# One-bank slot reads, two states loaded through GpSimd's queue, and a first layer fed head group by head group

## The chip, the cores and the metric

The kernel runs on one core of one Trainium2 chip. The core has TensorE (PE in the profile, with its weight loads as PEld), VectorE (DVE), ScalarE (ACT), GpSimd (POOL), SyncE (SP) and 16 DMA engines that all queues share. The metric is the device time of one execution in microseconds (us); lower is better.

## The reference, cut to what matters

Two stages follow each other. The first is an attention between 512 tokens and 32 state slots, for 8 batches and 8 heads of 64 numbers, read in both directions; the second is a two-layer perceptron over all 4352 rows that the first stage gives (8 batches of 512 tokens and 32 slots, 512 wide).

```python
scores  = scale * x @ state.T          # per batch and head: 512 x 32
a       = softmax(scores)              # over the 32 slots
xread   = a @ state                    # 512 x 64
scores2 = scale * state @ x.T          # 32 x 512
a2      = softmax(scores2)             # over the 512 tokens
sread   = a2 @ x                       # 32 x 64: the slot reads
rows    = concat(xread, sread)         # 544 rows a batch, heads side by side: 512 wide
h       = rows @ w_in                  # 512 -> 2048
g       = s * relu(h)**2 + b
out     = g @ w_out                    # 2048 -> 512
```

## The kernel before, in words

**Tiling.** Four heads lie together on the 128 partitions (32 slots each), in two groups g. Heads 2q+g belong to group g, so the two groups are the even and the odd heads. The token reads are never formed: since `xread @ w_in` is `a @ (state @ w_in)`, the kernel makes M = state x w_in for each batch and each quarter c of w_in (`att_M`; eight matmuls on tiles of 64 rows by 32 columns, then a cast of the 128x1024 result from PSUM to fp16 by ACT or DVE), and the first layer (`layer1`) multiplies M by the normalised scores a4. One "h" step of `layer1` is four matmuls into one pair of PSUM banks (two blocks f, and for each the two groups g), then a relu by ACT and a square by DVE. `layer2` works on sums and differences of blocks (`pair_sums` on the activations, `weight_sums` on w_out) in seven steps of eight parts; batch 0 goes through `layer2_first` without them.

**Scores.** For batch 0 x arrives in four pieces (`x0_load`, SP's queue), each piece is cast, transposed on TensorE and copied back; the states of batch 0 (`stf[0]`) and of batches 1 and 2 (`stf[1]`) come by two DMAs issued from ACT at lines 411 and 412, are cast by DVE (`att_st`) and transposed on TensorE. Score matmul, exp, a matmul with a block of ones for the sum over slots (D), ln, exp and a DVE product then give a4, for each group by itself. From batch 3 on a4 is made in another way: SP transposes exp(scores) by DMA into aT, DVE normalises it (`att_divide`) and SP transposes it back.

**Slot reads.** `part_V` (line 730) forms `a2 @ x` of one batch from aT and x: for each group, each of four token blocks c and each of four column parts q there are two matmuls, one for token rows 0 to 63 and one for rows 64 to 127, on tiles of 64x32, 64 columns long, into two PSUM banks. That is 64 matmuls. ACT or DVE copies the first bank (`vt`), DVE adds the second (line 930) and multiplies by the reciprocal of the sum (line 936). SP transposes the result, POOL copies it to its place, and `layer1_slots` uses all batches together near the end.

**Order.** Nothing is ordered by a scheduler at run time: the table TURNS lists, for each of the five engines, the numbers of its operations in the order in which they are issued, and every engine works through its own list strictly in order. `Plan.order` merges the lists, chooses buffers, and puts idle matmuls on a zero tile (`fill`) into TensorE's modelled gaps in the first 20 us. Its durations and landing times are a model's inputs, not measurements. TensorE changes between three modes: full (128x128), tiled (64x32) and cols (128x32).

**Loads.** After a copy that waits for the small constant, POOL issues the large loads one after the other: w_in part 1, w_in part 0, x of batch 1, w_in 2, w_out 0, w_in 3, w_out 1, x of batch 4, w_out 2, w_out 3, x of batch 2. At most eight such loads are under way; the ninth waits for the first.

Of the kernel before, what the change touches and what calls it, by code (L numbers as in the profile page):

```python
# [10 lines left out]
FP32 = mybir.dt.float32  # L11
# [7 lines left out]
        26 28 24 34 30 32 47 35 38-39 57 59 49 83 86 80 178 77 180 65 51 67 182 89 92 106-107 118 114 186  # L19
        108 119 110-111 71 112 115-116 185 120 113 98 117 126 95 109 122 230 127 123 227 124 215 128-129 221  # L20
        125 224 142-144 138-139 73 101 140-141 218 145 121 130 158 236 104 154-157 159-161 134 75 69 135 131
        136-137 132 54 1044 323 133 150 146 62 147 233 260 326-327 151 261 251 148 262 152 252 149 253 263
        153 254 162 264 255 163 350 166 265 167 338 344 256 164 266 1051 267 168-169 332 257-258 165 341 353
        270-272 687 438 273 347 335 279-281 274-275 282 276-277 1058 560 443 283-286 288-292 447 445 689 293
        298 294 299 295 300-304 563 569 441 308-312 305 313-315 565 1065 682 377 368-369 378-379 370-372 380
        373 381-382 472 454 374-375 383 475 469 384 387 460 388-391 463 392-393 457 396-400 394 401-403 1079
        567 685 405-412 415 466 416 425-426 582 427 585 417-418 579 419-421 428-429 1072 932 430 422 588 594
        431 490 432 597 591 491-492 499 576 500 707 493 501 494-496 502-503 497 504-505 691 804 928 506
        509-516 518-522 527 523-524 528 813 925 529 525 530-534 704 537 547-550 538-539 551 540 713 552 541
        553 719 542 701 554 543-544 716 621 698 612-614 622 615 623-624 616-619 710 625 838 626 631 627 841  # L30
        628 930 934 632-635 640 636-638 641-643 811 807 649 644-645 650 646 651 647 652-656 809 1086 1093
        659 669-671 660 672 661 673-674 662-663 675 820 664-665 676 835 826 734-738 666 829 739 743 740 744
        741 832 745-749 753-754 750 755-758 947 759-760 762-763 823 764-766 771-773 767-769 774-776 950 781
        777 782-783 778 784-788 791-794 956 953 856-857 795 858 796 859 797 944 798 860 1110 861 865-866 962
        867 941 862 868 863 1105 869-870 875 871-872 876-879 1115 880-881 884 882 885-889 893-894 890
        895-896 891 959 897-899 903-906 900 907 1100 908-910 913-919 1120 920 1130 977-978 1125 1135 986
        979-982 987 983-984 988-992 996 993 997-1003 1005-1011 1014 1012 1015-1021 1024-1031 1034-1041
        1152-1159 1161-1168 1171-1178 1180-1187 1189-1196 1199-1206 1209-1216
    """,
    "ACT": """  # L40
        27 29 21 36 33 37 40 43 41 44 60 84 87 81 78 66 183-184 90 93 190-191 72 187-188 99 96 231 228 216
        222 225 74 102 219 237 70 55 1046 325 324 63 328-329 234 351 339 345 333 342 354 688 440 439 348 336
        444 561-562 448 690 446 564 570 442 1067 683-684 566 473 455 476 470 461 458 464 686 467 568 586 583
        580 933 589 595 592 598 708 577 805-806 929 814 692 926-927 714 705 720 702 717 699 711 839 931 935
        842 808 812 1095 810 821 836 830 827 833 948 824 951 957 954 945 963 942 1111 1116 1108 1106 960
        1113 1103 1101 1121 1123 1118 1131 1136 1126 1128 1133 1138
    """,
    "DVE": """
        19-20 23 46 25 22 31 48 58 42 45 61 50 179 88 181 79 68 53 52 82 91 85 192 205 94 189 6 203 207 217
        229 7 223 204 100 1045 232 97 103 226 245 242 220 105 170 172 76 209 56 1047 64 238-239 208 318 199  # L50
        1048 1052 330 240 200 235 210 243 248-249 241 202 213 250 211 352 1059 1053 176 1054 206 259 174
        1055 246 268 212 244 201 343 340 355 334 214 349 278 1060 247 1061 337 287 1062 450-451 296 452 306
# [3 lines left out]
        587 489 1080 816 610 817-818 555 545 721 706 603 709 608 601 718 620 700 1083 712 715 604 731 629  # L56
# [5 lines left out]
        1160 1142 1169 1151 1179 1188 1148 1197 1207 1217  # L62
    """,
    "POOL": """
        8 10 9 15 12 11 14 13 437 16-18 197 193 195 322 559 171 269 317 307 803 386 681 414 177 175 424 536
        434 556 508 546 678 1078 173 297 1064 1085 1050 668 1092 1099 1057 1071 752 630 874 658 902 912 800
        780 922 790
    """,
# [229 lines left out]
def kernel(  # L298
# [10 lines left out]
    nc = tc.nc  # L309
# [414 lines left out]
    def V_bank(b, m):  # L724
        return T(("V", b))[:, m]
# [696 lines left out]
```

## Time and profile before

| what | value |
|---|---|
| median of the runs shown | 210.18 us (208.64 to 210.22, 3 runs) |
| the profiled execution | 209.36 us, of which its span is 207.6 us |
| PE, DVE, ACT, POOL busy, share of the span | 97%, 79%, 55%, 18% |
| first matmul of the first layer | 14.63 us from the span's start |
| last matmul | ends at 203.58 us |

The span runs from the first to the last instruction of the profiled execution; what lies around it makes the rest of its time. Times in views count from the span's start. A busy TensorE here is one with matmuls in its pipeline, so small steps can be stretched without showing as idle.

### The profile page before, as it was taken

Reading aid. Unit: us, or ns where it says so; the run is one execution under the profiler, and the core shown is the slowest. Engines: PE = TensorE matmul, PEld = TensorE weight load, DVE = VectorE, ACT = ScalarE, POOL = GpSimd, SP = SyncE. Lnnn points to the kernel's source line nnn. Section 1 sums busy time; section 2 is a strip of 40 time slices with the busy share of each in tenths; the row PEclk is TensorE's granted clock in tenths of the full one; section 3 lists DMA queues with packets and bytes.
Section 4 is the critical chain, followed back from the end, with each engine's and each line's share of the span. In section 5 each row is a group of like instructions: output and inputs, shape, how many; then the busy total and the mean of one; then the engine's idle time right before and its main releaser. Section 6 shows DMA issues by size and latency. Waiting matters only on the chain.

```text
span 207.6 us, 5286 instructions
## 1 busy us (share of the span) xinstructions
PE 200.6 (97%) x2240; PEld 136.3 (66%) x2240; DVE 164.6 (79%) x334; ACT 114.0 (55%) x158; POOL 37.6 (18%) x59
## 2 busy tenths in 40 slices
PE   7799999999999999999999999999999999999992
PEld 4655444446557685676568756686777778888881
DVE  3466836979999879888989979996798756899671
ACT  3468987656577986548675595743532541340000
POOL 5821002010030040302100230003750002160000
PEclk9999999999999999999999999999999999999998
DMA  5999999979999749999902255004402003152054
GB/s 167 228 205 203 204 205 155 181 140 141 175 131 209 132 104 180 113 178 217 195 0 54 101 100 165 3 3 106 164 6 101 3 0 103 54 176 81 0 192 113
DMA packets 47768, 25.87 MB, mean 125 GB/s; under 512 B 32128, under 2 KB 45952, under 8 KB 47744
## 3 DMA queue, kind: packets, MB, share of 16 engines
q0 software_dynamic: 13744, 15.21, 36.6%
q1 hardware_dynamic: 33056, 10.10, 25.8%
q8 instruction: 17, 0.28, 0.6%
q10 hardware_dynamic: 944, 0.23, 0.5%
q14 instruction: 7, 0.06, 0.1%
HBM read 17.33 MB, written 8.91 MB: 126 GB/s over the span
## 4 chain that ended last, share of the span: by engine, by line
PE 93%; DMA 3%; DVE 1%; ACT 0%; ACTq 0%; issue 0%
PE o L336 50%; PE pair L336 43%; DMA stf<-in_state_dram 3%; ACT M L425 0%; DVE st L425 0%; DVE xn L425 0%; ACTq L411 0%; DVE osb L1273 0%; ACTq L410 0%; DVE stT L425 0%
## 5 line engine op out<-in xcount | busy, mean ns | idle before, releaser
L999 ACT ACTIVATE g<-pair 128x1024 f16<-128x1024 f32 x64 | 63.5, 1023 | 41.5 <-PE pair L336 41.2
L336 PE MATMUL pair<-a,M 128*128 128x512 f16 x256 | 63.9, 379 | 0.5 <-ACT M L425 0.5
L336 PEld LDWEIGHTS <-pd 128*128 128x128 f16 x480 | 46.3, 98 | 10.9 <-issue 2.3
L336 PEld LDWEIGHTS <-g 128*128 128x128 f16 x424 | 40.7, 98 | 18.4 <-issue 2.6
L1005 DVE TENSOR_TENSOR g<-g 128x1024 f16<-128x1024 f16 x64 | 42.5, 687 | 2.7 <-ACT g L999 2.7
L336 PE MATMUL o<-u,pd 128*128 128x256 f16 x360 | 44.4, 273 | 0.0
L336 PE MATMUL o<-wo,g 128*128 128x256 f16 (+1 forms) x272 | 42.9, 285 | 0.0
L336 PEld LDWEIGHTS <-M 128*128 128x128 f16 x256 | 24.7, 98 | 23.0 <-ACT M L425 1.0
L1176 POOL DMA_DIRECT2D out_dram<-osb x28 | 18.9, 744 | 98.9 <-DVE osb L1284 55.8
L1273 DVE SCALAR_TENSOR_TENSOR osb<-o,s,bias_bc 128x512 f32<-128x512 f32 (+1 forms) x32 | 22.9, 716 | 12.6 <-PE o L336 11.2
L425 ACT CAST M<-pair 128x1024 f16<-128x1024 f32 x24 | 23.6, 1015 | 9.6 <-PE pair L336 9.4
L1284 DVE SCALAR_TENSOR_TENSOR osb<-o,s,osb 128x512 f32<-128x512 f32 (+1 forms) x24 | 17.2, 715 | 7.5 <-PE o L336 7.2
L1085 DVE TENSOR_TENSOR pd<-g 128x1024 f16<-128x1024 f16 (+1 forms) x32 | 20.4, 651 | 0.1
L336 PE MATMUL o<-wo,pd 128*128 128x256 f16 x120 | 17.9, 273 | 0.0
L336 PE MATMUL o<-u,g 128*128 128x256 f16 x120 | 17.5, 273 | 0.0
L1096 DVE TENSOR_TENSOR pd<-g,pd 128x512 f16<-128x512 f16 (+1 forms) x32 | 12.8, 400 | 0.0
L1093 DVE TENSOR_TENSOR pd<-g,pd 128x512 f16<-128x512 f16 (+1 forms) x32 | 12.3, 402 | 0.1
L780 ACT ACTIVATE E<-pair 128x512 f16<-128x512 f32 x16 | 9.4, 598 | 3.1 <-PE pair L336 3.1
L466 POOL DMA_DIRECT2D xn<-in_x_dram x7 | 6.6, 949 | 22.8 <-ACT vt L425 10.7
L336 PE MATMUL pair<-wo,g 128*128 128x512 f16 x32 | 10.5, 380 | 0.0
L1046 ACT ACTIVATE g<-pair 128x256 f16<-128x256 f32 x16 | 5.2, 386 | 9.0 <-PE pair L336 9.0
L336 PE MATMUL pair<-wi,stT 64*32 64x512 f16 x224 | 10.0, 382 | 0.0
(72 smaller groups left out, 147.7 us busy)
## 6 DMA issues: line engine op xcount, KB each, us to landing
out_dram<-osb POOLq DMA_DIRECT2D x28, 256.0 KB, 3.4
xn<-in_x_dram POOLq DMA_DIRECT2D x7, 512.0 KB, 10.7
wi<-in_moe_w_in_dram POOLq DMA_DIRECT2D x4, 512.0 KB, 9.1
wo<-in_moe_w_out_dram POOLq DMA_DIRECT2D x4, 512.0 KB, 19.4
u<-in_x_dram SPq DMA_DIRECT2D x4, 256.0 KB, 4.2
out_dram<-osb SPq DMA_DIRECT2D x4, 256.0 KB, 2.7
out_dram<-osb SPq DMA_DIRECT2D x4, 128.0 KB, 2.3
pd<-in_state_dram SPq DMA_DIRECT2D x1, 320.0 KB, 3.8
```

Of the source, the lines that this page charges most:

```text
L336: return nc.tensor.matmul(out, lhsT, rhs, start=start, stop=stop, tile_position=tp, is_transpose=is_transpose, skip_group_check=True,)
L425: (nc.scalar.copy if e == "ACT" else nc.vector.tensor_copy)(dst, src)
L466: lambda e: nc.gpsimd.dma_start(out=T(xn[b]).rearrange("p h c d -> p h (c d)"), in_=x[b].rearrange("h (q c) d -> q h (c d)", q=P),),
L780: nc.scalar.activation(T(E[b])[:, g, :].rearrange("p (m t) -> p m t", m=2), T(u)[:, :, hS * g : hS * g + hS], AF.Exp, scale=scale, accum_o ...
L999: lambda e, u=u, part=part: nc.scalar.activation(part(), T(u), AF.Relu),
L1005: lambda e, part=part: nc.vector.tensor_mul(part(), part(), part()),
L1085: nc.vector.tensor_tensor(view()[:, :, 0:2], blocks(b, j)[:, :, 1:2, :].to_broadcast((P, 2, 2, n)), blocks(b, j)[:, :, 0:4:3, :], ALU.subt ...
L1093: nc.vector.tensor_tensor(view()[:, :, 2], blocks(b, j)[:, :, 3], view()[:, :, 0], ALU.subtract)
L1096: nc.vector.tensor_tensor(view()[:, :, 3], blocks(b, j)[:, :, 2], view()[:, :, 2], ALU.subtract)
L1176: lambda e: eng(e).dma_start(dst, src()),
L1273: lambda e: nc.vector.scalar_tensor_tensor(t_view(u), o_view(bank), s_bc, bias(h), ALU.mult, ALU.add),
L1284: lambda e: nc.vector.scalar_tensor_tensor(t_view(u), o_view(bank), s_bc, t_view(u), ALU.mult, ALU.add),
```

## The change

Four things are changed in the code, and the TURNS table is rewritten for all engines.

1. **Slot reads.** `part_V` drops the split of the token rows: 32 matmuls over all 128 rows on tiles of 128x32, into one bank. The copy into `vt` and the addition fall away (16 instructions in 8 batches), and the product with the reciprocal reads PSUM directly.
2. **States of batches 1 and 2.** The DMA for `stf[1]` leaves ACT's queue (line 412) and becomes an operation of POOL's list, behind w_in 0.
3. **Order of the loads.** POOL's list becomes w_in 0, `stf[1]`, x of batch 1, w_in 1, w_out 0, w_in 2, w_out 1, w_in 3, w_out 2, w_out 3, x of batch 2, x of batch 3. The x of batch 4 follows after slot reads of batch 0 have freed its buffer.
4. **First layer of batch 0.** For the first two quarters of w_in the cast of M is split by group (128x512 each), and an h step is split into two steps of two matmuls, one for each group, so that the even heads' step waits only for the even heads' M and a4.

In the new lists ACT casts the first, second and fourth pieces of x of batch 0 and DVE the third (before: DVE the first, second and fourth, ACT the third). TensorE starts the first layer with quarter 0 of w_in (before: quarter 1), and one product M stands ahead of it instead of three. DVE casts four whole M of batches 6 and 7 that ACT cast before (seven whole and six half casts of M on DVE in all, before four and five). The lists of the middle and the end are permuted throughout.

```diff
     "POOL": """
-        8 10 9 15 12 11 14 13 437 16-18 197 193 195 322 559 171 269 317 307 803 386 681 414 177 175 424 536
+        8-9 11 16 10 12-15 17-19 329 200 204 202 444 566 180 304 314 276 393 688 810 1060 421 441 182 431
...
-    plan.buffers("vt", [sb(f"vt_{i}", [NG * D], FP32) for i in range(2)])
...
-    nc.scalar.dma_start(stf[1], st_v[:, NG : NS * NG, :])
...
     wi_load(1)
+    op(
+        {"POOL": 0.9},
+        lambda e: nc.gpsimd.dma_start(out=stf[1], in_=st_v[:, NG : NS * NG, :]),
+        rd=[g0],
+        wr=[K(("stf", 1))],
+        dma=("sw", 0.45),
+    )
...
-            rd=[K(stf2)] if i == 2 else [],
+            rd=[[], [K(("stf", 1))], [K(stf2)]][i],
...
-                    for m in range(2):
-                        rows = slice(64 * m, 64 * m + 64)
-                        mm(
-                            V_bank(b, m)[32 * q : 32 * q + 32, D * g : D * g + D],
-                            T(aT[b])[rows, g, c, 32 * q : 32 * q + 32],
-                            T(xn[b])[rows, 2 * q + g, 2 * (c % 2) + c // 2, :],
-                            start=(c == 0 and g == 0),
-                            stop=(c == SCH - 1),
-                            tp=(64 * m, 32 * q),
-                        )
+                    mm(
+                        V_bank(b)[32 * q : 32 * q + 32, D * g : D * g + D],
+                        T(aT[b])[:, g, c, 32 * q : 32 * q + 32],
+                        T(xn[b])[:, 2 * q + g, 2 * (c % 2) + c // 2, :],
+                        start=(c == 0 and g == 0),
+                        stop=(c == SCH - 1),
+                        tp=(0, 32 * q),
+                    )
...
-            mode="tiled",
+            mode="cols" if kind == "V" else "tiled",
...
+        if b == 0 and c < 2:
+            for g in range(NG):
+                op(
+                    {"ACT": 0.48, "DVE": 0.64},
+                    lambda e, g=g: copy(e, T(M[b, c])[:, g], T(u)[:, g]),
+                    rd=[K(u)],
+                    wr=[K(M[b, c], g)],
+                )
+            return
...
-        vt = plan.unit(("vt", b), "vt")
-        op(
-            {"ACT": 0.27, "DVE": 0.25},
-            lambda e: copy(e, T(vt), V_bank(b, 0)[:, 0 : NG * D]),
-            rd=[V_key(b)],
-            wr=[K(vt)],
-        )
-        op(
-            {"DVE": 0.25},
-            lambda e: nc.vector.tensor_add(T(vt), V_bank(b, 1)[:, 0 : NG * D], T(vt)),
...
-                T(vt).rearrange("p (g d) -> p g d", g=NG),
+                V_bank(b)[:, 0 : NG * D].rearrange("p (g d) -> p g d", g=NG),
...
-                op(
-                    {"PE": 0.865},
-                    h,
-                    rd=[K(M[b, j], g) for g in range(NG)]
-                    + [K(a4[b], g) for g in range(NG)],
+                for gg in [[g] for g in range(NG)] if b == 0 and j < 2 else [range(NG)]:
+                    op(
+                        {"PE": 0.4325 * len(gg)},
+                        lambda e, h=h, gg=gg: h(e, gg=gg),
+                        rd=[K(M[b, j], g) for g in gg] + [K(a4[b], g) for g in gg],
```

More of the change, by code (lines that the diff above doesn't have):

```diff
@@ L24 @@
[L24 to L28, printed above, removed]
@@ L447, in x0_load @@
             dma=("hw", 0.75),
-            lands=(3.6, 4.85, 6.0, 6.55)[i],
+            lands=(3.6, 4.7, 6.0, 6.5)[i],
         )
@@ L598, in att_st @@
             ),
-            rd=[K(stf2)] if i == 2 else [],
+            rd=[[], [K(("stf", 1))], [K(stf2)]][i],
             wr=[key],
-            since=(5.2, 6.6, 0.0)[i],
+            since=(5.0, 0.0, 0.0)[i],
         )
@@ L722, in part_M, with V_bank @@
                 )
-    def V_bank(b, m):
-        return T(("V", b))[:, m]
+    def V_bank(b):
+        return T(("V", b))[:, 0]
     def V_key(b):
@@ L941, in ev @@
             )
-        op({"DVE": 0.2}, ev, rd=[K(vt), K(rs[b], "r")], wr=[K(sr[b])])
+        op({"DVE": 0.25}, ev, rd=[V_key(b), K(rs[b], "r")], wr=[K(sr[b])])
         op(
@@ L969, in layer1, with h @@
                 fs = range(2 * p, 2 * p + 2)
-                def h(e, j=j, fs=fs, u=u):
+                def h(e, j=j, fs=fs, u=u, gg=range(NG)):
                     for i, f in enumerate(fs):
-                        for g in range(NG):
+                        for g in gg:
                             mm(
@@ L980, in h @@
                             )
-                op(
-                    {"PE": 0.865},
-                    h,
-                    rd=[K(M[b, j], g) for g in range(NG)]
-                    + [K(a4[b], g) for g in range(NG)],
-                    wr=[K(u)],
-                    mode="full",
-                    into=[G[b, j]],
-                    mms=4,
-                )
+                for gg in [[g] for g in range(NG)] if b == 0 and j < 2 else [range(NG)]:
[3 more added lines that the diff above has]
+                        rd=[K(M[b, j], g) for g in gg] + [K(a4[b], g) for g in gg],
+                        wr=[K(u)],
+                        mode="full",
+                        into=[G[b, j]],
+                        mms=2 * len(gg),
+                    )
                 gk = K(G[b, j], p)
```

84 lines of the change are left out of this document (42 added, 42 removed), and 7 rows, old and new, of the table TURNS.

## The prediction

> **What bounds the kernel now.** I read the page first, then TensorE's waits, then the chain of waits, and last the timeline of the first 27 us.
>
> ```profile
> span 207.6 us, 5286 instructions
> PE 200.6 (97%) x2240; PEld 136.3 (66%) x2240; DVE 164.6 (79%) x334; ACT 114.0 (55%) x158; POOL 37.6 (18%) x59
> ...
> PE 93%; DMA 3%; DVE 1%; ACT 0%; ACTq 0%; issue 0%
> ```
>
> TensorE fills 97% of the span and 93% of the chain that ended last. Its own waits on other engines are few:
>
> ```profile
> PE pair L336 <- DVE stT L425: 1.2, 1, 1.2
> ...
> PE pair L336 <- ACT M L425: 0.5, 1, 0.5
> ```
>
> So after the start the end is set by how much time TensorE's steps take, and before that by when it can begin. The head of the chain shows what it begins with, and its last row what follows TensorE:
>
> ```profile
> 1.77 6.15 DMA stf<-in_state_dram
> 7.95 0.76 DVE st L425
> 8.71 0.19 DVE stT L425
> ...
> 203.61 0.48 DVE osb L1273
> ```
>
> The load of the states of batches 1 and 2 lands at 7.92. DVE's list holds their cast ahead of the small copy `stT` of batch 0, which was ready much earlier; everything for batch 0 stands behind it.
>
> ```profile
> 4.92 0.65 DVE L425 CAST st<-stf 128x256 f16<-128x256 f32 x1
> ...
> 9.33 0.60 ACT L780 ACTIVATE E<-pair 128x512 f16<-128x512 f32 x1 [1.84 <-PE pair L336]
> ...
> 14.55 0.58 ACT L425 CAST M<-o 128x512 f16<-128x512 f32 x1 [0.77 <-PE o L336]
> ...
> 14.63 1.68 PE L336 MATMUL pair<-a,M 128*128 128x512 f16 x7
> ```
>
> The first exp starts at 9.33 and the first layer at 14.63. From there TensorE runs to 203.6 with two gaps: 0.41 of idle matmuls on the zero tile (19.09 to 19.5) and 0.49 before 21.06:
>
> ```profile
> 19.09 0.49 PE L336 MATMUL o<-warm 128*128 128x256 f16 x3
> ...
> 21.06 1.90 PE L336 MATMUL pair<-a,M 128*128 128x512 f16 x8 [0.49 <-ACT M L425]
> ```
>
> **The change part by part.** *Slot reads.* The lone slot read of batch 1 and the bias sum, which already uses 128x32 tiles, carry the price:
>
> ```profile
> 55.41 0.38 PE L336 MATMUL o<-wo,g 128*128 128x256 f16 x2
> 55.72 0.76 PE L336 MATMUL pair<-xn,aT 64*32 64x64 f16 x64
> 56.41 0.39 PE L336 MATMUL o<-wo,g 128*128 128x256 f16 x2
> ...
> 55.72 0.57 PEld L336 LDWEIGHTS <-aT 64*32 64x32 f16 x64 [0.21 <-issue]
> ...
> 35.86 0.41 PE L336 MATMUL pair<-wi,stT 64*32 64x512 f16 x8
> 36.20 1.05 PE L336 MATMUL pair<-wo,ones 128*32 128x512 f16 x16
> 37.18 0.61 PE L336 MATMUL o<-wo,g 128*128 128x512 f16 x2
> ```
>
> From 55.72 to 56.41 are 0.69 us. The 64 weight loads take 0.57 of it, and about 0.12 is the change back to full mode. In the bias sum 37.18 - 36.20 - 0.12 = 0.86 for 16 matmuls of 512 columns, four at a time: 0.215 a round, so a 128x32 round of 64 columns streams in 0.027. The old read has eight rounds on eight tiles, the new one eight rounds on four: both stream 8 x 0.027 = 0.215. The old one takes 0.57, so something other than streaming sets it. If it is issue, 0.57/64 = 8.9 ns a pair, the new read costs 32 x 8.9 ns = 0.28; if it is each tile's own eight pairs in turn (71 ns each), it stays 0.57. These are the ends, with 0.215 as the floor. One more row decides between them:
>
> ```profile
> 55.70:55.80 0.10, 0.08 (x19) 0.08 (x24) 0.00 (x0) 0.00 (x0) 1.00 0.89 177
> ```
>
> In the first 0.08 us 24 pairs' weight loads begin, three for each tile; a tile is not held for 71 ns by a pair. I take 0.28: 8 x (0.57 - 0.28) = **2.3 us less** on TensorE. It is on the path, because nothing covers TensorE's steps.
>
> The new read is in the cols mode, so it no longer joins its tiled neighbours free of charge. A change from tiled to cols costs 0.34 - 0.215 = about 0.12 (35.86 to 36.20, less one M product; the last three M products of a row stand 0.22 apart). Counted through the two lists, TensorE changes mode 45 times before and 50 times after; the isolated stretches that leave the full mode are 22 in both, and the five extra changes are between tiled and cols: 5 x 0.11 = **0.55 us more**. No row shows a change from full to cols; the nearest, full to tiled, is 55.41 + 2 x 0.108 (half of 0.215 for 256 columns) = 55.63 to 55.72 = 0.09, and I use the same.
>
> The Trainium skill, in "TensorEngine Tiling (Array Packing)", section Tiling Modes, says that changing the tiling mode drains the engine, which speaks against this part; the trace agrees, with 0.09 to 0.12 a change.
>
> The `vt` copy and addition go, from ACT and DVE. They lie beside TensorE's work and give it no time; DVE takes four whole casts of M instead (weighed below).
>
> *The first layer's start.* Here I follow ACT's list, since it is the tightest. Landings by the trace's DMA view:
>
> ```profile
> u<-in_x_dram SPq DMA_DIRECT2D x1, 256.0 KB, 5.1
> ...
> u<-in_x_dram SPq DMA_DIRECT2D x2, 256.0 KB, 5.3
> ...
> stf<-in_state_dram ACTq DMA_DIRECT2D x1, 64.0 KB, 3.6
> ```
>
> The third piece of x lands at 1.75 + 5.1 = 6.85, the fourth (the second of the row with two, median 5.3) at 2.27 + 5.5 = 7.8, the states of batch 0 at 1.17 + 3.6 = 4.8. With the wait of 7.92 gone, the fourth piece is late next: DVE casts the third by 7.3, copies `stT` by 7.6, the score matmul of the even heads is done by 8.0, and ACT, which now casts the fourth piece first (0.62), starts exp at 8.4 instead of 9.33. From there ACT has a chain without holes but one:
>
> ```profile
> 11.05 0.60 ACT L780 ACTIVATE E<-pair 128x512 f16<-128x512 f32 x1 [0.39 <-PE pair L336]
> 11.55 0.19 ACT L780 ACTIVATION_READ_ACCUMULATOR E<-pair 128x1 f32 x1
> 11.64 1.15 ACT L815 ACTIVATE o<-o 128x512 f32<-128x512 f32 x2
> 12.70 1.08 ACT L821 ACTIVATE a<-o 128x512 f16<-128x512 f32 x2
> ```
>
> exp with its accumulator 0.68, a wait of 0.35 for the D matmul, ln 0.55, exp 0.68, a = exp 0.54, ln 0.55, half of M 0.52, a = exp 0.54, other half of M 0.52: 8.4 + 4.9 = 13.3, and 0.2 to reach TensorE: 13.5 against 14.63, **1.1 us earlier**. By then only one M product is done instead of three, so two of 0.22 follow: **0.43 more**. Splitting the h steps adds no matmul; its waits for the odd half end earlier than TensorE gets there (the odd M half is cast first), so I give the split nothing beyond the earlier start. If the 128 KB no longer on ACT's queue let the fourth piece land sooner, up to 0.4 more is won; if it lands later, as much is lost.
>
> *The loads.* TensorE now asks for w_in 1 behind x of batch 1. Three rows give the beat and the new load's price:
>
> ```profile
> wi<-in_moe_w_in_dram POOLq DMA_DIRECT2D x1, 512.0 KB, 7.5
> ...
> wo<-in_moe_w_out_dram POOLq DMA_DIRECT2D x1, 512.0 KB, 20.5
> ...
> q10 hardware_dynamic: 944, 0.23, 0.5%
> ```
>
> The first load lands at 2.90 + 7.5 = 10.4; w_out 2, the ninth, at 10.66 + 20.5 = 31.2: 2.6 us a load. Queue 10 (the constant and both state loads) spends 0.005 x 207.6 x 16 / 944 = 17.6 ns on a packet of about 250 bytes; the 128 KB are 512 of these on 16 engines: 0.56 us. So in the new order w_in 1 lands at 10.4 + 0.56 + 2 x 2.6 = 16.2, w_out 0 at 18.8, w_in 2 at 21.4, w_out 1 at 24.0, w_out 2 at 29.2. Adding TensorE's steps in its new order from 13.5 on, it asks for these at 16.4, 18.7, 21.2, 24.1 and 29.1. That is even, with no slack, and T of batch 1 and the split casts hold it some 0.5 us near 17. I put 0.9 us of gaps there, the same as the 0.41 + 0.49 of before: **nothing net**.
>
> **Sum:** -2.3 + 0.55 - 1.1 + 0.43 = -2.4 us. The profiled execution took 209.36 (207.6 and 1.76 around it), so it would give 207.0; it lies 0.8 under the median of the runs, 210.18. I forecast from the median: 210.18 - 2.4 = 207.8, and as the rows shown lean to the better end (the floor of 0.215, an earlier fourth piece), I say **207.6**. Own range 206.6 to 208.6.
>
> **The rivals.** *The queue holds the whole read.* The burst at 55.70 (24 loads in 0.08 us, 3.3 ns each) lasts through all 32 pairs, and streaming alone is left: 0.215 a read, 8 x 0.065 = 0.5 better: 207.1. For it speaks that row; against it, a read right behind another step shares the queue with it. The Trainium skill, "TensorE: Matmul & The Clock Gate", on the array of 16 sub-arrays and queue depths, states a queue of 64 instructions for TensorE, which 32 pairs would just fill.
>
> *Each tile's own pairs set the pace,* as weighed above: 0.57 stays, 2.3 is not won: 209.9. The Trainium skill ("TensorEngine Tiling (Array Packing)", Performance Considerations) gives each matmul an overhead of about 60 cycles whatever its length. By that, as an estimate, a read would cost 8 x (64 + 60) cycles = 0.41 at the 2.4 GHz it gives, and the sum would be about 1.0 worse.
>
> *TensorE's steps are moved ahead of what they need.* In the first 30 us each of five loads is asked for when it lands, and the a4 of batch 4 comes back by SP's transposes with about 1.4 us to spare (its DVE product ends near 80.5, the first h step of batch 4 would be at 85.4). The rows for such a transpose, alone and beside a load of x:
>
> ```profile
> a<-aN SPq DMA_TRANSPOSE x1, 3.1
> ...
> a<-aN SPq DMA_TRANSPOSE x1, 6.4
> ```
>
> At 6.4 it is 1.5 too late; half a us of later loads has a like price: 209.1.
>
> *DVE becomes the bound between 100 and 140 us.* This is the case that ends slower. DVE takes four whole casts of M there:
>
> ```profile
> 100.00:120.00 20.00, 20.00 (x196) 14.07 (x195) 18.84 (x38) 12.12 (x19) 2.06 (x3) 1.00 0.29 74
> 120.00:140.00 20.00, 20.00 (x302) 14.22 (x301) 18.29 (x35) 12.78 (x14) 2.08 (x3) 1.00 0.29 70
> ...
> L425 DVE CAST M<-pair 128x1024 f16<-128x1024 f32 x4 | 4.9, 1218 | 1.5 <-PE pair L336 1.5
> ...
> L930 DVE TENSOR_TENSOR vt<-pair,vt 128x128 f32<-128x128 f32 x8 | 2.2, 278 | 0.2 <-ACT vt L425 0.2
> ```
>
> They are 4 x 1.22 = 4.9 us; idle are 1.16 + 1.71 = 2.9, and the additions and copies removed there free about 0.8. It decides from the point where 4.9 exceeds 3.7 and what the new list moves out of the stretch; the full price, if every cast delays an eviction that TensorE's banks wait for, is 4.9: 212.5. Against it: the list does move squares and pair sums past 140, and adding DVE's steps up against TensorE's I find no eviction over 1.2 us late, about as in the order of before.
>
> **How the numbers follow.** The sum as worked 0.42 (207.6); the queue holds the read 0.14 (207.1); tiles set the pace 0.12 (209.9); steps ahead of their inputs 0.18 (209.1); DVE bound 0.14 (212.5). One per cent of 210.18 is 2.1 us, about what a measurement of this kernel can tell from no change: faster than 208.08 or slower than 212.3. The forecast lies under 208.08 in some three quarters of its own range, the first rival nearly always, the others hardly: 0.32 + 0.13 + 0.05 = 0.50 faster; slower is most of the last rival and a remainder, 0.13; 0.37 within. The range runs from the forecast with both better ends (206.6 less 0.8) to the price of a partly bound DVE: 205.8 to 211.6.
>
> **What would show it.** The first layer's first matmul near 13.5; exp at 8.4 and no DVE wait for the states; a lone slot read of about 0.28 of weight loads instead of 0.57; TensorE's waits still under about 1 us after 14; DVE's waits for TensorE not gone between 100 and 140; last matmul near 201. It is wrong if a slot read keeps 0.57, if TensorE shows waits for w_in or w_out loads in the first 30 us, or if it waits for DVE's `osb` or `pd` later on.

## The result, and the profile after

| what | before | after |
|---|---|---|
| median in the comparison | 210.13 us (20 runs) | 208.11 us (20 runs) |
| ratio after : before | | 0.9927, 95% interval 0.9902 to 0.9953 |
| the same comparison on another chip | 209.28 us (23 runs) | 207.57 us (11 runs); ratio 0.9913, 0.988 to 0.9945 |
| the profiled execution, and its span | 209.36 us, 207.6 | 208.01 us, 206.2 |
| first matmul of the first layer | 14.63 us | 13.81 us |
| last matmul ends | 203.58 us | 202.19 us |

The change makes the kernel 0.7% to 0.9% faster: 1.5 us by the first ratio (0.0073 x 210.1), 1.8 by the second. Both intervals lie below 1. The forecast was 207.6 us, 2.4 to 2.6 faster. The ratios are taken over undisturbed executions, the medians over all. Before has medians of 208.7 to 210.1 us on different chips, so times below are compared within one chip only.

The page of the profile after, its first lines and the shares of the chain that ended last:

```profile
span 206.2 us, 4768 instructions
...
PE 199.3 (97%) x1989; PEld 134.7 (65%) x1989; DVE 164.3 (80%) x325; ACT 109.3 (53%) x153; POOL 38.8 (19%) x60
...
PE 89%; DMA 7%; DVE 1%; issue 0%; ACT 0%; POOL 0%; DVEq 0%
```

TensorE still fills the span and the chain, with 251 matmuls fewer (8 x 32 by the reads, less 5 idle ones added: 58 before, 63 after). The share of DMA in the chain has grown from 3% to 7%. The chain's DMA rows and the last step say where (start, length):

```profile
0.75 2.48 DMA ident<-ident_const
...
3.41 8.27 DMA wi<-in_moe_w_in_dram
...
70.81 3.87 DMA out_dram<-osb
...
202.21 0.48 DVE osb L1270
```

Before, the chain began with the states of batches 1 and 2 (to 7.92). Now it begins with the small constant that GpSimd waits for and the first load of w_in, which lands at 11.68. TensorE's waits for other engines (total, times, longest):

```profile
PE pair L335 <- DMA wi<-in_moe_w_in_dram: 1.2, 1, 1.2
...
PE pair L335 <- DVE sr L933: 0.3, 1, 0.3
```

The wait for `stT` (1.2) and that for M (0.5) are gone; one for the first part of w_in (1.2) and one for a slot read's product (0.3) are new. The start, from ACT's and TensorE's timelines:

```profile
7.52 0.60 ACT L782 ACTIVATE E<-pair 128x512 f16<-128x512 f32 x1
...
11.72 0.41 PE L335 MATMUL pair<-wi,stT 64*32 64x512 f16 x8 [1.21 <-DMA wi<-in_moe_w_in_dram]
...
13.81 1.04 PE L335 MATMUL pair<-a,M 128*128 128x512 f16 x4
...
17.08 0.50 PE L335 MATMUL pair<-warm 128*128 128x256 f16 x3
...
18.07 0.72 PE L335 MATMUL pair<-warm 128*128 128x256 f16 x5
18.64 2.19 PE L335 MATMUL pair<-a,M 128*128 128x512 f16 x8
```

The first exp starts at 7.52 instead of 9.33, 1.8 earlier, but the first layer only 0.8 earlier, because the first M product had to wait for w_in at 11.72. Behind it stand eight idle matmuls on the zero tile (three at 17.08, five at 18.07); before had three in that stretch. Idle matmuls can hide a wait, since TensorE counts as busy while it runs them. What goes on beside them (all engines' timeline, last row from the chain):

```profile
17.51 0.41 PE L335 MATMUL pair<-wi,stT 64*32 64x512 f16 x8
17.73 0.87 POOL L463 DMA_DIRECT2D xn<-in_x_dram  x1 [1.73 <-DMA wi<-in_moe_w_in_dram]
18.00 0.59 ACT L422 CAST M<-pair 128x512 f16<-128x512 f32 x1 [0.57 <-PE pair L335]
18.61 0.69 DVE L422 CAST M<-pair 128x512 f16<-128x512 f32 x1 [1.08 <-ACT M L422]
...
19.36 0.82 PE pair L335 x3
```

The second part of w_in to be used (w_in 1, issued at 5.94) lands at 17.45. The product M made from it starts at 17.51, right behind the three idle matmuls, and GpSimd's issue at 17.73 was waiting for the same load. ScalarE then casts one half of M and VectorE the other, one after the other and not side by side. The step on the second half can start only at 19.36: the row of 18.64 takes 2.19 for eight matmuls that take 1.90 elsewhere, and holds a wait of 0.3 that the waits view leaves out. So the idle matmuls stand where TensorE would have waited, first for the load and then for the casts.

The slot reads, those that tell most:

```profile
47.92 0.42 PE L335 MATMUL pair<-xn,aT 128*32 128x64 f16 x32
48.27 0.41 PE L335 MATMUL o<-wi,stT 64*32 64x512 f16 x8
...
47.92 0.29 PEld L335 LDWEIGHTS <-aT 128*32 128x32 f16 x32 [0.42 <-issue]
...
108.61 0.70 PE L335 MATMUL pair<-xn,aT 128*32 128x64 f16 x64
109.24 1.92 PE L335 MATMUL o<-u,pd 128*128 128x256 f16 x16
```

A read with the change behind it takes 0.35 (47.92 to 48.27), so 0.23 without the 0.12 of the change; its weight loads take 0.29, where the old ones took 0.57. Two reads in a row take 0.63 - 0.12 = 0.51, or 0.255 each. How the weight loads begin, in the new lone read at 47.92 and in the old one at 55.72 (stretch, length, busy time and number of weight loads in it, then clock, DMA share, GB/s):

```profile
47.92:48.04 0.12, 0.12 (x20) 1.00 0.00 0
```

```profile
55.72:55.83 0.11, 0.11 (x32) 1.00 0.76 149
```

In the old read 32 loads begin in 0.11 us; its other pairs follow at 8.3 ns each. In the new one 20 begin in 0.12: by the starts in the trace its rounds of four stand 29 ns apart (the first 40), near the 27 that 64 columns take to stream. Only in two reads in a row do the rounds widen to 33 ns, 8.3 ns a pair, from about the eleventh on.

In the timeline of before, two reads next to tiled neighbours stand like this:

```profile
136.47 0.41 PE L336 MATMUL pair<-wi,stT 64*32 64x512 f16 x8
136.70 1.28 PE L336 MATMUL pair<-xn,aT 64*32 64x64 f16 x128
137.91 0.39 PE L336 MATMUL o<-wo,pd 128*128 128x256 f16 x2
```

They take 1.21, or 0.545 each without the change. Summed over all eight reads, with the mode changes next to them, the timeline of before gives 0.57 + 0.69 + 0.49 + 0.53 + 0.50 + 0.50 + 1.21 (two) = 4.5 us, that of after 0.35 + 0.34 + 0.46 + 0.47 + 0.63 (two) + 0.63 (two) = 2.9: **1.6 us less**. This leaves out that some steps behind an old read run longer, by 0.3 in all (the score matmuls behind the reads at 44.43 and 74.75 take 0.43 up to the next step, elsewhere 0.33).

Last, VectorE between 100 and 140 us (stretch, length, then busy time and instructions of TensorE, its weight loads, VectorE, ScalarE and GpSimd, then clock, DMA share, GB/s):

```profile
100.00:120.00 20.00, 20.00 (x257) 14.24 (x256) 19.02 (x35) 10.52 (x17) 2.69 (x5) 1.00 0.61 128
120.00:140.00 20.00, 20.00 (x243) 14.25 (x241) 18.64 (x32) 9.43 (x10) 2.50 (x5) 1.00 0.37 106
```

VectorE is busy for 37.7 of 40 us, 0.5 more than before, and TensorE has no wait for it there.

### The profile page after: what moved, and what is told of

It is laid out like the page before. It is cut to its first block, busy times and chain, and to the rows that moved or that the text cites. A ratio compares the mean times of both kernels' runs of the same rounds, so it can differ in the third digit from the quotient of the medians.

```text
span 206.2 us, 4768 instructions
## 1 busy us (share of the span) xinstructions
PE 199.3 (97%) x1989; PEld 134.7 (65%) x1989; DVE 164.3 (80%) x325; ACT 109.3 (53%) x153; POOL 38.8 (19%) x60
## 4 chain that ended last, share of the span: by engine, by line
PE 89%; DMA 7%; DVE 1%; issue 0%; ACT 0%; POOL 0%; DVEq 0%
PE o L335 48%; PE pair L335 41%; DMA wi<-in_moe_w_in_dram 4%; DMA out_dram<-osb 2%; DMA ident<-ident_const 1%; DVE osb L1281 0%; DVE M L422 0%; ACT M L422 0%; DVE osb L1270 0%; DVE aN L906 0%; DVE sr L933 0%; POOL gate L552 0%; DVEq L1270 0%
## 5 line engine op out<-in xcount | busy, mean ns | idle before, releaser
L422 ACT CAST M<-pair 128x1024 f16<-128x1024 f32 (+1 forms) x22 | 20.4, 958 | 7.8 <-PE pair L335 7.8
L335 PE MATMUL o<-wo,pd 128*128 128x256 f16 x120 | 19.0, 273 | 0.0
L422 DVE CAST M<-pair 128x1024 f16<-128x1024 f32 (+1 forms) x8 | 9.2, 1153 | 4.9 <-PE pair L335 3.8
L1093 DVE TENSOR_TENSOR pd<-g,pd 128x512 f16<-128x512 f16 (+1 forms) x32 | 12.5, 400 | 0.1
L1090 DVE TENSOR_TENSOR pd<-g,pd 128x512 f16<-128x512 f16 (+1 forms) x32 | 12.1, 400 | 0.1
```

Of the source, the lines that this page charges most:

```text
L335: return nc.tensor.matmul(out, lhsT, rhs, start=start, stop=stop, tile_position=tp, is_transpose=is_transpose, skip_group_check=True,)
L422: (nc.scalar.copy if e == "ACT" else nc.vector.tensor_copy)(dst, src)
L1090: nc.vector.tensor_tensor(view()[:, :, 2], blocks(b, j)[:, :, 3], view()[:, :, 0], ALU.subtract)
L1093: nc.vector.tensor_tensor(view()[:, :, 3], blocks(b, j)[:, :, 2], view()[:, :, 2], ALU.subtract)
```

## The experiments

Three marks are read from each timeline: the start of the first layer, that of the bias sum, and the end of the last matmul. Ahead of the bias sum stands the same amount of TensorE's work in both orders: 81 products of 512 columns of both layers and 7 products M after the change, 80 and 8 before, and a product M (0.22) takes as long as one of the others.

| kernel | first layer | bias sum | last matmul ends | bias sum to end |
|---|---|---|---|---|
| before | 14.63 | 36.20 | 203.58 | 167.38 |
| before, another execution | 13.27 | 35.12 | 202.54 | 167.42 |
| before with the new reads | 15.37 | 36.93 | 202.93 | 166.00 |
| before, cast of the states later | 13.99 | 35.52 | 202.93 | 167.41 |
| after | 13.81 | 36.67 | 202.19 | 165.52 |
| after, another execution | 12.49 | 35.21 | 200.64 | 165.43 |
| after with the old reads | 12.28 | 35.02 | 202.63 | 167.61 |
| after, first layer unsplit | 13.27 | 36.04 | 201.58 | 165.54 |
| after, early send | 12.70 | 35.42 | 200.60 | 165.18 |
| after, states on ACT's queue | 13.41 / 13.08 | 35.51 / 35.18 | 201.06 / 200.56 | 165.55 / 165.38 |
| the same with the early send | 12.52 / 12.68 | 35.49 / 35.33 | 200.67 / 200.50 | 165.18 / 165.17 |

Two things are seen at once. Behind the bias sum a list repeats itself within 0.2 us, so small effects can be read there. Ahead of it two executions of the same kernel differ by over 1 us (14.63 and 13.27; 13.81 and 12.49).

### The slot reads

The new reads alone, in the kernel before; the product with the reciprocal takes the place of the addition in VectorE's list:

```diff
-                    for m in range(2):
-                        rows = slice(64 * m, 64 * m + 64)
-                        mm(V_bank(b, m)[...], T(aT[b])[rows, ...], T(xn[b])[rows, ...], ..., tp=(64 * m, 32 * q))
+                    mm(V_bank(b)[...], T(aT[b])[:, ...], T(xn[b])[:, ...], ..., tp=(0, 32 * q))
...
-        vt = plan.unit(("vt", b), "vt")
```

> The kernel before with the one-bank reads alone; the product that evicts a read stands in DVE's list where the addition stood, all else as before. Theory A (TensorE's steps set the end, a read falls from 0.57 to about 0.23 us, 2.7 us in 8 reads, less about 0.5 us of added mode changes): 2.0 to 2.4 us faster than before, ratio 0.989 to 0.991, last matmul near 201.4 in the trace, first layer still near 14.6. Theory B (what the reads save is given back in waits on DVE's evictions or on output buffers, because the lists were fitted to the slower reads): less than 1 us faster, ratio over 0.995, with new waits of TensorE on DVE after 40 us.

Measured: ratio 0.9922, interval 0.9892 to 0.9953, or 1.6 us less than before (208.73 us there), between the two theories. The trace comes from a second run of the same kernel:

> The kernel before with the one-bank reads alone, once more for an undisturbed trace. Theory A: slot reads of 0.22 to 0.24 us without their mode changes, TensorE's step times otherwise as before, no wait of TensorE on DVE over 0.3 us, last matmul 2.0 us or more earlier than in the trace of before taken beside it. Theory B: 1 us or more of new waits of TensorE behind slot reads, on DVE's eviction or on the buffers that it frees.

Measured: 208.66 us in one execution, beside a median of 208.99 for before; bias sum to end 166.00. The lone read of batch 1 in this trace, whose row before is quoted in the prediction:

```profile
56.28 0.42 PE L335 MATMUL pair<-xn,aT 128*32 128x64 f16 x32
56.63 0.39 PE L335 MATMUL o<-wo,g 128*128 128x256 f16 x2
```

0.35 instead of 0.69. Reads next to tiled steps win less: they took 0.5 and no change, and now take 0.35 and a change of 0.1 ahead of them. Behind the bias sum 1.4 us are won. The reads with all changes of mode there give 1.7, and a new wait for a pair sum of VectorE takes 0.3 back (from the chain):

```profile
147.77 0.52 DVE pd L1075
148.29 0.05 issue
148.33 0.72 PE o L335 x5
```

So there is one wait of the kind that theory B has, of 0.3 us and not of 1 or more.

The other way round, the changed kernel with 64 matmuls of half height into two banks. It leaves out the addition of the second bank, so VectorE's work stays that of the change:

```diff
-                    mm(V_bank(b)[...], T(aT[b])[:, ...], T(xn[b])[:, ...], ..., tp=(0, 32 * q))
+                    for m in range(2):
+                        rows = slice(64 * m, 64 * m + 64)
+                        mm(T(("V", b))[:, m][...], T(aT[b])[rows, ...], T(xn[b])[rows, ...], ..., tp=(64 * m, 32 * q))
```

> The changed kernel with each slot read again as 64 matmuls of 64 rows in two banks; the second bank is left unread, so the slot rows miss half of their tokens and DVE's work stays that of the changed kernel. Theory A: the changed kernel loses 2.0 to 2.7 us, ratio to the kernel before 1.003 to 1.006. Theory B: it loses under 1 us, ratio under 0.998.

Measured: ratio to before 1.0063, interval 1.0039 to 1.0087; bias sum to end 167.61 against 165.52, **2.1 us more**. Without the new reads the change makes the kernel slower. Some of the 2.1 is a wait: the product of a slot read came later, and TensorE waited 0.5 for it near 75 us, where it waits 0.3 after the change. That leaves 1.8 to 1.9 for the reads themselves and their changes of mode.

```profile
75.29 0.41 PE L335 MATMUL pair<-wi,stT 64*32 64x512 f16 x8 [0.53 <-DVE sr L935]
```

### The start

Before, with VectorE's cast of the states of batches 1 and 2, and TensorE's transposes of them, moved behind what batch 0 needs; the load stays where it was:

```diff
 "DVE"
-        26 28 24 34 30 32 47 35 38-39 57 59 49 ...
+        26 28 24 34 30 32 35 38-39 47 57 59 49 ...
 "PE"
-        19-20 23 46 25 22 31 48 58 42 45 61 50 ...
+        19-20 23 25 22 31 46 48 58 42 45 61 50 ...
```

> The kernel before with DVE's cast of the states of batches 1 and 2 (and TensorE's transposes of them) moved behind what batch 0 needs; all else as before. It takes the wait for the state load away from batch 0. Theory A (in the order before the loads leave about 1 us of room): first exp near 8.4 at the latest, first layer 13.3 to 13.8, and 0.6 to 1.0 us faster than before, ratio 0.995 to 0.997. Theory B (the start is held by a load anyway, then an earlier start turns into waits for w_in 0 or w_in 2): first layer earlier but the last matmul within 0.3 us of before, ratio 0.998 to 1.001.

Measured: ratio 0.9999, interval 0.9981 to 1.0018. ACT starts exp at 7.60 in this trace, so the wait for the states is out of the way, and nothing is won, as theory B had it. The three products M ahead of the first layer suggest why:

```profile
10.90 0.41 PE L336 MATMUL pair<-wi,stT 64*32 64x512 f16 x8
11.24 1.37 PE L336 MATMUL pair<-warm 128*128 128x256 f16 x11
12.55 0.41 PE L336 MATMUL o<-wi,stT 64*32 64x512 f16 x8
12.89 0.83 PE L336 MATMUL pair<-warm 128*128 128x256 f16 x6
13.65 0.41 PE L336 MATMUL pair<-wi,stT 64*32 64x512 f16 x8
13.99 2.76 PE L336 MATMUL pair<-a,M 128*128 128x512 f16 x12
```

The first layer comes right behind the last of them. By this trace, freeing the chain of batch 0 is worth something only together with the products moved out from in front of the first layer; moving them alone was not tried.

The kernel before once more, for the spread of its start:

> The kernel before once more, for a second trace of its start. Theory A (the first layer's start at 14.6 in the first trace was an execution in which the state load landed late; the time of the change's front lies in the loads): here the states land near 7.3 instead of 7.9 and the first layer starts near 14.0, held by w_in 0, so moving the cast behind can win nothing. Theory B (the late state load is how this kernel always starts): 7.8 to 8.0 and 14.5 to 14.7 again.

Measured: 208.28 us. VectorE's cast of the states could start at 7.08 instead of 7.95, and the first layer started at 13.27 instead of 14.63: the start that the prediction took for the kernel's was that of one execution.

The changed kernel with the first layer of batch 0 whole again (M of quarter 0 cast by ACT, of quarter 1 by DVE):

```diff
-        if b == 0 and c < 2:
-            for g in range(NG):
-                op({"ACT": 0.48, "DVE": 0.64}, ..., T(M[b, c])[:, g], T(u)[:, g], ...)
-            return
...
-                for gg in [[g] for g in range(NG)] if b == 0 and j < 2 else [range(NG)]:
+                for gg in [range(NG)]:
```

> The changed kernel with the first layer of batch 0 unsplit: whole casts of M, by ACT for quarter 0 and by DVE for quarter 1, and h steps of four matmuls. Theory A (the split gives only what the two engines win by sharing the casts): 0.2 to 0.5 us slower than the changed kernel, ratio to the kernel before 0.993 to 0.996. Theory B (starting on the even heads is what the new front rests on): 0.8 us or more slower, ratio 0.997 or more.

Measured: ratio 0.994, interval 0.9914 to 0.9967, where the change has 0.9927 and 0.9913. By these the split is worth 0.6 us at most, and nothing that could be told from none. The trace gives 0.35: the bias sum starts 19.50 behind the product M on w_in 1, and 19.15 with the split (table in the next part).

### The states' queue, and a late send

The changed kernel with the states of batches 1 and 2 on ACT's queue again. The planner then takes them to land sooner, and puts fewer idle matmuls into TensorE's list:

```diff
+    nc.scalar.dma_start(stf[1], st_v[:, NG : NS * NG, :])
...
-    op(
-        {"POOL": 0.9},
-        lambda e: nc.gpsimd.dma_start(out=stf[1], in_=st_v[:, NG : NS * NG, :]),
-        ...
-    )
...
-            rd=[[], [K(("stf", 1))], [K(stf2)]][i],
+            rd=[[], [], [K(stf2)]][i],
```

> The changed kernel with the states of batches 1 and 2 loaded by ACT's queue at the start, as before; the order of the large loads, the lists and the reads are those of the change. Theory A (the new front is held by when w_in 0 and the later loads land, and the state load between them costs each later one about 0.6 us): w_in 1 and all later loads land 0.5 to 0.7 earlier relative to w_in 0, and the kernel is 0.3 to 0.7 us faster than the changed one, ratio 0.990 or a little under. Theory B (the front is held by the pieces of x of batch 0, which the state load on ACT's queue delays): the first exp comes 0.5 us or more later than 7.5, the kernel is as slow as the changed one or slower, ratio 0.993 to 0.996.

Measured: ratio 0.9895, interval 0.9863 to 0.9928. On top of this, the send of a block of the output moved ahead of two other sends in GpSimd's list (a text below calls them gathers; in the trace without the move they are the sends at 69.68 and 72.94):

```diff
 "POOL"
-        ... 565 179 303 313 275 392 687 ...
+        ... 565 179 275 303 313 392 687 ...
```

> The changed kernel with the states loaded by ACT's queue, and POOL's store of the first block of batch 1 moved ahead of the two that stand before it and become ready some 12 us later. Theory A (TensorE's wait of 0.3 near 75 us comes from an output buffer that this store frees too late): the wait of 1.3 us of DVE on the store and TensorE's 0.3 us behind it go, ratio to the kernel before 0.987 to 0.990. Theory B (another store or another buffer holds it): the same waits again, ratio as with the states alone, 0.989 to 0.991.

Measured: ratio 0.9878, interval 0.9847 to 0.991. To compare these with the change itself, all four were then run on one chip (before: 209.28 us):

> The changed kernel as it stands, beside the three below on one chip. Theory A (the reads give about 2.1 us behind the bias sum, the start gives next to nothing on average, the write-back of the output takes 0.3 back): ratio 0.991 to 0.994, and bias sum to last matmul again 165.5 us. Theory B (the first comparison happened to miss part of a gain at the start of 0.7 to 1.1 us): 0.988 to 0.990.

> The changed kernel with the states of batches 1 and 2 loaded through ACT's queue, as before. Theory A (moving the load to GpSimd's queue costs time: the first x and w_in transfers share the engines with it, whichever queue issues it, and GpSimd's list is longer by one issue): about 0.3 us below the changed kernel of this comparison, ratio 0.988 to 0.991. Theory B (the queue makes no difference that repeats): within 0.1 us of the changed kernel.

> As the one before, and the send of a finished output block of batch 1 is moved ahead of two gathers in GpSimd's list. Theory A: the stretch behind the bias sum ends 0.35 earlier, 165.2 instead of 165.55, so about 0.35 us below the one before and 0.4 to 0.7 below the changed kernel. Theory B (the early send collides with a load and the gain is lost in other executions): no difference from the one before.

> The changed kernel with that send moved alone, the states on GpSimd's queue. Theory A: bias sum to last matmul 165.15 instead of 165.5, VectorE's wait for the output transfer near 74 us gone, and about 0.35 us below the changed kernel. Theory B (TensorE's 0.3 us wait near 75.8 has another cause): the wait stays and the time does not move.

| kernel | median | ratio to before |
|---|---|---|
| the change | 207.57 | 0.9913 (0.988 to 0.9945) |
| states on ACT's queue | 206.48 | 0.9855 (0.9814 to 0.9895) |
| the same, early send | 206.46 | 0.9854 (0.9813 to 0.9894) |
| the change, early send | 208.61 | 0.993 (0.9888 to 0.9971) |

**The states.** The two with the states on ACT's queue lie 1.1 us under the change, more than the 0.3 expected: of their twelve executions ten took 206.2 to 206.6, of the eleven of the change one. The first layer starts no later with that queue: 13.41, 13.08, 12.52 and 12.68, against 13.81, 12.49 and 12.70. What differs is behind its start. There most traces with the split are held by the same thing, the load of w_in 1. The second execution of the change, with idle matmuls ahead of the product on it:

```profile
15.56 0.50 PE L335 MATMUL pair<-warm 128*128 128x256 f16 x3
16.06 0.41 PE L335 MATMUL pair<-wi,stT 64*32 64x512 f16 x8
...
16.30 0.88 POOL L463 DMA_DIRECT2D xn<-in_x_dram  x1 [2.63 <-DMA wi<-in_moe_w_in_dram]
```

The first trace with the states on ACT's queue and the early send, without them:

```profile
15.25 0.41 PE L335 MATMUL o<-wi,stT 64*32 64x512 f16 x8
16.34 0.41 PE L335 MATMUL pair<-wi,stT 64*32 64x512 f16 x8 [0.68 <-DMA wi<-in_moe_w_in_dram]
```

All traces with the split (idle matmuls: those between first layer and bias sum; the last column is bias sum less product):

| kernel | w_in 1 lands behind w_in 0 | w_in 1 lands | product on it | idle | to the bias sum |
|---|---|---|---|---|---|
| after | 5.77 | 17.45 | 17.51 | 8 | 19.16 |
| after, another execution | 6.48 | 16.02 | 16.06 | 8 | 19.15 |
| after, early send | 5.67 | 16.23 | 16.27 | 8 | 19.15 |
| after with the old reads | 5.89 | 15.82 | 15.86 | 8 | 19.16 |
| after, states on ACT's queue | 5.15 / 5.15 | 15.84 / 15.75 | 16.36 / 16.03 | 2 | 19.15 / 19.15 |
| the same with the early send | 5.91 / 5.59 | 16.30 / 16.14 | 16.34 / 16.18 | 2 | 19.15 / 19.15 |

In six of the eight traces the product starts within 0.07 of the landing, with the idle matmuls or without, and from it to the bias sum takes 19.15 in all eight, with eight idle matmuls or two. So here the idle matmuls cost nothing: they fill the wait for w_in 1 and that for the casts of M. In the other two the load was there 0.3 to 0.5 before TensorE came to the product, 2.95 behind the start of the first layer; an earlier first layer than that is waited out at w_in 1.

The queue changes when w_in 1 lands: with the states between them on GpSimd's queue it comes 6.0 behind w_in 0 in the mean of four, without them 5.5, and the prediction's price for that load was 0.56. That can account for half of the 1.1. The rest shows in no trace: the profiled execution of the change on this chip was its fastest (206.44). In all traces of the changed lists with the new reads and the split, the execution's time is the start of that product plus 190.0 to 190.5, so the slower executions of the change (a median of 207.57) probably had w_in 1 a us later, as the first trace did (17.45 and 208.01). That is argued, and not shown.

**The send.** In the changed kernel VectorE waits at 74.80 for a buffer that the output's transfer still reads, the product of a slot read stands behind that, and TensorE waits for it (all engines' timeline):

```profile
74.06 1.38 POOL L1173 DMA_DIRECT2D out_dram<-osb  x2 [2.57 <-ACT M L422]
...
74.80 0.75 DVE L1270 SCALAR_TENSOR_TENSOR osb<-o,s,bias_bc 128x512 f32<-128x512 f32 x1 [1.29 <-DMA out_dram<-osb]
...
75.47 0.28 DVE L933 TENSOR_TENSOR sr<-pair,rs 128x128 f16<-128x128 f32 x1
...
75.81 0.41 PE L335 MATMUL pair<-wi,stT 64*32 64x512 f16 x8 [0.27 <-DVE sr L933]
```

With the early send these waits are gone and bias sum to end is 165.17 or 165.18 in all three traces, 0.2 to 0.4 under the lists without it. The times don't show it: 206.46 us against 206.48 on ACT's queue, and a ratio of 0.993 against 0.9913 on GpSimd's. An effect of this size is below what these comparisons tell.

The version with the states on ACT's queue is faster than before in both comparisons (1.1% and 1.5%), and lies 1.1 us under the change on the one chip where both ran (206.48 us); the early send adds nothing that could be measured.

## Why the prediction was right, and where it was off

The forecast (faster by 2.4 to 2.6 us, 207.6) had the sign and the main mechanism right, the cheaper slot reads, and was about 1 us too good: 1.5 and 1.8 were measured. That is less than the 1% which the prediction gave one chance in two; it falls to its 0.37 for a smaller change.

**The sum by the marks,** each the mean of the two traces of before and of the change: first layer -0.8, first layer to bias sum +1.1, bias sum to the end -1.9; together -1.6. The prediction's terms for these were -1.1, +0.43 and -1.75. So the reads came out a little better than forecast, the start a little worse, and the stretch between them lost 0.65 more.

**Slot reads, forecast -2.3 + 0.55 = -1.75.** The timelines give -1.6 to -1.9, as the slower steps behind the old reads are left out or counted. The new reads alone give -1.6 by the ratio and -1.4 by the trace, with a wait of 0.3 in it, and the old ones put back 2.1 in the changed lists, again with 0.3 of waits. The sum was right, its two parts less so. A new read costs 0.23 to 0.255 rather than 0.28. But an old one next to tiled steps cost 0.5, not 0.57, since the next tiled step starts in its tail. That the errors cancel is luck. *Each tile's own pairs set the pace* has fallen: 0.57 would have stayed. The Trainium skill's overhead of about 60 cycles for each matmul ("TensorEngine Tiling (Array Packing)", Performance Considerations), added to the 64 columns, would be 0.41 a read as an estimate and does not agree with the 0.23 measured. *The queue holds the whole read* (0.215) is what a lone read does: rounds 29 ns apart, where the forecast's 8.9 ns a pair would have put them 36 apart. The forecast's pace a pair, 8.3 measured, shows only where two reads follow each other.

**The first layer's start, forecast -1.1.** The first trace shows 13.81 instead of 13.5, -0.8. Two executions of one kernel differ by more than that (14.63 and 13.27; 13.81 and 12.49), and the prediction read the start off a single one. Its working named the wrong limit in this execution: ACT's chain from the fourth piece of x. That piece came early (exp at 7.52, not 8.4), and the first load of w_in, expected at 10.4, landed at 11.68. The beat forecast for the loads behind it held; they all came 0.9 to 1.3 later. That the queue of the states is not what brings the first layer forward is shown by the variants with ACT's queue (13.41, 13.08, 12.52, 12.68). That the order of the casts and the one product M ahead do it together is read from the traces, and the product was not tried alone.

**Two products M behind the start, forecast +0.43, and the gaps, "nothing net".** This is the step that failed. From first layer to bias sum before takes 21.57 and 21.85, the change 22.86 and 22.72. Between the shorter ones, 1.15 more, 0.43 is the two products. The prediction had w_in 1 at 16.2 and TensorE asking for it at 16.4, "even, with no slack". TensorE does come to it 2.95 behind the first layer, as the prediction's 13.5 and 16.4 say. But the load landed 3.5 to 3.6 behind the first layer in the two traces of the change, so TensorE was held there for 0.6 to 0.75, under cover of the three idle matmuls. Then the two halves of M were cast one after the other, 1.85 from the product to the step on the second half (the prediction had allowed 0.5 for T of batch 1 and the casts). Up to that step the change loses 0.5 more than before lost in its gaps (0.41 + 0.49) and the changes of mode beside them. The last 0.2 is one more stretch out of the full mode further on, at the prediction's own 0.09 and 0.12. TensorE leaves the full mode five times between first layer and bias sum, three times before; the other of the two lies within the 0.5 and comes from the idle matmuls. The prediction had counted these stretches over the whole list, 22 in both, and left the idle matmuls out.

**What the prediction didn't have.** The wait for the output's transfer near 74 us, worth about 0.3. And the move of the states as a cost: the prediction had priced the load itself (0.56) in the landing of w_in 1, and allowed 0.4 either way for the 128 KB leaving ACT's queue; against ACT's queue the runs give a loss of 1.1 us on the one chip where it was compared, perhaps half of it in the landings above.

**The other rivals.** *DVE becomes the bound*: VectorE takes on the four casts of M and is busy for 37.7 of 40 us between 100 and 140, and TensorE never waits for it there. *TensorE's steps moved ahead of what they need* came in part: in the first trace a wait for w_in of 1.2 ahead of the first layer and one for w_in 1 behind it that the idle matmuls cover; for the transposes of batch 4 there is no wait (by its own 3.1 the prediction had 1.8 us to spare there, not 1.4).

## What to carry to other kernels

A long row of short matmuls is paid by the pair, not by the column: half as many pairs over twice the rows took about half the time here, and a lone row of 32 pairs came near the time of its columns, even where it brought mode changes. Idle matmuls hide waits: TensorE counts as busy in them, and the waits view is silent. Before counting them as a cost, look at when the step behind them had its inputs; here six fewer of them left the bias sum where the load had put it. An earlier start is worth no more than the next landing allows. And a start that hangs on the first DMA landings has to be read from several executions: one trace of before was 1.4 us later than another, as much as the change was to win there.

## What the runs showed of the hardware

The landing of the first transfers varies between executions of the same program. GpSimd's copy, which waits for the small constant, and the first issue behind it, in the two traces of the changed kernel:

```profile
3.29 0.18 POOL L552 COPY gate<-ident 128x2 f16<-128x2 f16 x1 [2.84 <-DMA ident<-ident_const]
...
11.96 0.86 POOL L487 DMA_DIRECT2D wo<-in_moe_w_out_dram  x1 [2.16 <-DMA wi<-in_moe_w_in_dram]
```

```profile
2.50 0.19 POOL L552 COPY gate<-ident 128x2 f16<-128x2 f16 x1 [2.05 <-DMA ident<-ident_const]
...
9.82 1.59 POOL L487 DMA_DIRECT2D wo<-in_moe_w_out_dram  x2 [0.91 <-DMA wi<-in_moe_w_in_dram]
```

The 32 KB of the constant landed 0.8 us later in the one, and the load of w_out that waits for the first w_in to land could be issued 2.1 us later. The first layer started 1.3 later, and these executions took 208.01 and 206.44 us. A load is in only when the last of its 16 parts is: in the slower trace fifteen parts of the first w_in were there at 9.59 and the last at 11.68, and the product that waits for it started at 11.72; in the other trace they were there at 9.29 and 9.54.

The pace of short pairs over a long row is nearly the same on both kinds of tiles: 128 pairs on eight tiles of 64x32 took 1.09 us (8.5 ns a pair), 64 pairs on four tiles of 128x32 took 0.51 (8.0 ns). Twice as many tiles at work gave no faster pace. The first 32 pairs are not held to it: on eight tiles their weight loads began 3.3 ns apart, and on four tiles rounds of four started every 29 ns (7.3 ns a pair), later ones every 33.
